# Cached multi-head attention on one core: steps of four heads, two batches at once in the projections, p scaled before a bf16 transpose

## The chip, the core and the metric

The kernel runs on one core of a Trainium2 chip. A core has TensorE (PE, matrix products into PSUM), VectorE (DVE) and ScalarE (ACT) for the work on rows, GpSimd (POOL, here only for an identity matrix), and SyncE (SP), whose queue issues all transfers (DMAs) between the device's memory and the on-chip SBUF. The engines work side by side; each works through its own list in order and waits on semaphores for the others. The metric is the device time of one execution in microseconds (us); lower is better.

## The reference

Eight batches of 112 queries attend to cached keys and values of 32 heads. Keys and values come as they are; q and the output are projected.

```python
B, Sq, D = 8, 112, 640
H, Sk, Dh = 32, 512, 192          # x, k_cache, v_cache, wq, wo are bf16
q = (x @ wq).reshape(B, Sq, H, Dh).transpose(0, 2, 1, 3)
scores = einsum("bhqd,bhkd->bhqk", q, k_cache) * (Dh ** -0.5)
p = softmax(scores, axis=-1)
o = einsum("bhqk,bhkd->bhqd", p, v_cache)
return o.transpose(0, 2, 1, 3).reshape(B, Sq, H * Dh) @ wo     # (8, 112, 640)
```

## The kernel before

**Tiling.** The heads are taken in four groups of eight (HG = 8), and one group of one batch is a *unit*: 32 units, group by group, batch by batch. A unit's keys arrive by a transposing DMA in `kt` (three buffers), its values by a plain DMA in `vt` (three buffers), each 1536 KB. Four keys at a time lie in one row of 768 numbers, so that a head's 192 channels are cut at 128-channel borders: chunk 0 holds channels 0 to 127 of the even keys, chunk 2 channels 64 to 191 of the odd keys, and chunk 1 the last 64 of the even ones in its lower half beside the first 64 of the odd ones in its upper half. A unit is worked off in four *pairs* of heads, 128 pairs in all.

**A pair's stages.** On PE: Q (L210, fifteen products of 112 columns, one batch), S (L137 to L140: per head four products of 256 columns; for chunk 1, L138 and L140, the q operand has zeros in the other half's rows, so each is a full product), PT0 and PT1 (L153: p transposed by a product with a diagonal matrix `dg` that holds 1/sum, so that p is normalised in the same product; output f32), PV (L171 for 128 channels of each head, L178 for the other 64 of both heads, side by side in the two column halves of the array), O (L194 and L195: o as weights, `wo` as the moving operand of 512 and 128 columns, accumulated over a unit in PSUM). On DVE: smax (L265, scaled copy of the scores with the row minimum of their negative), qc (L256 to L259, four copies that arrange q for the chunks), the evacuation of the second transposed p (L271), recip (L277), two diag (L249), and once a unit the sum over head groups (L291 to L295). On ACT: the evacuation of q (L220), of the first transposed p (L226), the two exps (L232, with the row sums), the evacuation of o (L239).

**Order.** `DEFAULT_ORDERS` gives each engine's list of stages with lags: in iteration i PE does S of pair i, PT of pair i−1, PV of pair i−2, O of pair i−3 and Q of pair i+2. SP issues per unit K, V and one weight load (L336, L344, L354 or L361; 480 KB), each K and V after the unit three back has given up its buffer; x comes batch by batch (L347). The last eight units have no weight load behind them. The outputs are stored at the end (L396).

Of the kernel before, what the change touches and what calls it, by code (L numbers as in the profile page):

```python
# [11 lines left out]
DEFAULT_ORDERS = dict(  # L12
    PE=[("S", 0), ("PT0", -1), ("PV", -2), ("PT1", -1), ("O", -3), ("Q", 2)],
    ACT=[("evacQ", 1), ("evacpT0", -1), ("exp0", 0), ("exp1", 0), ("evacPV", -2)],
    DVE=[("smax0", 0), ("smax1", 0), ("qc", 1), ("evacpT1", -1), ("recip", 0), ("diag0", 0), ("diag1", 0),
         ("oacc", -3)],
)


def build_mha_kernel(nc, x, k_cache, v_cache, wq, wo, out, cfg=None):  # L20
    cfg = dict(cfg or {})
    B, SQ, D = x.shape
    _, H, SK, DH = k_cache.shape
    assert SQ == 112 and D == 640 and SK == 512 and DH == 192
    assert H % 4 == 0
    HD = H * DH
    DC = D // 128
    HG = cfg.get("HG", 8 if H % 8 == 0 else 4)
    assert H % HG == 0 and HG % 4 == 0
    NHG = H // HG  # L30
    PPU = HG // 2
    NUNIT = NHG * B
    NPAIR = NUNIT * PPU
    scale = float(DH) ** -0.5

    def unit_of(ip):
        u, lp = divmod(ip, PPU)
        hg, b = divmod(u, B)
        return u, hg, b, lp

    NB = 3
    NQ = cfg.get("NQ", 3)
    NSS = cfg.get("NSS", 4)
    NP = cfg.get("NP", 4)
    ND = cfg.get("ND", 4)
    NPT = cfg.get("NPT", 3)
    NO = cfg.get("NO", 3)
    NS = 8
    QJ = [0, 2, 1, 3]
    orders = dict(DEFAULT_ORDERS)  # L50
    orders.update(cfg.get("orders", {}))
    lags = [lag for o in orders.values() for _, lag in o]
    PER = range(-max(lags), NPAIR - min(lags))

    EA = [0, 5]
    OC = [4, 2]
    ET = [7, 6]
    OH = [3, 8]
    NSLOT = 9

    with ExitStack() as es:
# [3 lines left out]
        def sem(name):  # L65
            return es.enter_context(nc.semaphore(name))

        WQC = HG * DH
        wq_sb = sb("wq_sb", [128, 2, DC, WQC], BF16)
        wo_sb = sb("wo_sb", [128, 2, 3 * PPU, D], BF16)  # L70
        acc = sb("acc", [SQ, B, D], F32)
# [3 lines left out]
        qs = sb("qs", [128, NQ, NSLOT, SQ], BF16)  # L75
        s_sb = sb("s_sb", [SQ, NSS, SK], F32)
        p_sb = sb("p_sb", [SQ, NP, SK], BF16)
        dg = sb("dg", [SQ, ND, SQ], BF16)
        pT_sb = sb("pT_sb", [128, NPT, 2, 4 * SQ], BF16)
        oT_sb = sb("oT_sb", [128, NO, 3, SQ], BF16)  # L80
        o_out = sb("o_out", [SQ, B, D], BF16)
        ident = sb("ident", [128, 128], BF16)
        nmx = sb("nmx", [SQ, NS], F32)
        rsum = sb("rsum", [SQ, NS], F32)
        rinv = sb("rinv", [SQ, NS], F32)
        ps = es.enter_context(nc.psum_tensor("ps", [128, 8, 512], F32))

        sS = sem("sS"); sPT = sem("sPT"); sPV = sem("sPV"); sO = sem("sO"); sQ = sem("sQ")
        dSM = sem("dSM"); dDG = sem("dDG"); dQC = sem("dQC"); dPTE = sem("dPTE"); dOA = sem("dOA"); dRC = sem("dRC")
        aEX = sem("aEX"); aQE = sem("aQE"); aPTE = sem("aPTE"); aPVE = sem("aPVE")  # L90
        gI0 = sem("gI0"); gINIT = sem("gINIT"); dINIT = sem("dINIT")
        mX = [sem(f"mX{j}") for j in range(B)]
        dummy = sb("dmy_act", [SQ, 4], F32)
        mK = [sem(f"mK{j}") for j in range(NB)]
        mV = [sem(f"mV{j}") for j in range(NB)]
        mK0 = sem("mK0b"); mV0 = sem("mV0b")
        mOUT = [sem(f"mOUT{j}") for j in range(2)]

        mWQ = [sem(f"mWQ{j}") for j in range(3 * PPU)]
        mWO = [sem(f"mWO{j}") for j in range(3 * PPU)]  # L100

        def wsem(lst, hg, lp):
            return lst[lp if hg == 0 else (1 + hg % 2) * PPU + lp]

        def wcount(hg):
            return 16 if hg == 0 else 16 * ((hg + 1) // 2)

        HALF = PPU // 2

        def kv_wait(eng, sems, first2, u, lp):  # L110
            if u == 0 and lp >= HALF:
                W(eng, first2, 16)
            else:
                W(eng, sems[u % NB], 16 * (u // NB + 1))

        block = es.enter_context(nc.Block())

        def W(eng, s, v):
            if v > 0:
                eng.wait_ge(s, v)  # L120

        def ok(ip):
            return 0 <= ip < NPAIR

        def pe_S(pe, i):
            u_, hg, b, lp = unit_of(i)
            qb = i % NQ
            W(pe, dQC, i + 1)
            kv_wait(pe, mK, mK0, u_, lp)
            for h in range(2):  # L130
                Hh = 2 * i + h
                u = Hh % HG
                W(pe, dSM, Hh - 1)
                bk = ps[0:SQ, h, :]
                ktb = kt[u_ % NB]
                cs = slice(u * 128, (u + 1) * 128)
                pe.matmul(bk[:, 0:256], qs[:, qb, EA[h], :], ktb[:, :, 0, cs], start=True, stop=False)  # L137
                pe.matmul(bk[:, 0:256], qs[:, qb, ET[h], :], ktb[:, :, 1, cs], start=False, stop=True)  # L138
                pe.matmul(bk[:, 256:512], qs[:, qb, OC[h], :], ktb[:, :, 2, cs], start=True, stop=False)  # L139
                pe.matmul(bk[:, 256:512], qs[:, qb, OH[h], :], ktb[:, :, 1, cs], start=False, stop=True).then_inc(sS, 1)  # L140

        def pe_PT(pe, ip, h):
            Hh = 2 * ip + h
            W(pe, aEX, Hh + 1)
            W(pe, dDG, Hh + 1)
            if h == 0:
                W(pe, aPTE, ip)
            else:
                W(pe, dPTE, ip)
            pslot = Hh % NP  # L150
            dslot = Hh % ND
            for j in range(4):
                mm = pe.matmul(ps[:, 2 + h, j * SQ:(j + 1) * SQ], p_sb[:, pslot, j * 128:(j + 1) * 128],  # L153
                               dg[:, dslot, :], start=True, stop=True)
            mm.then_inc(sPT, 1)

        def pe_PV(pe, ip):
            u_, hg, b, lp = unit_of(ip)
            ptb = ip % NPT
            W(pe, aPTE, ip + 1)  # L160
            W(pe, dPTE, ip + 1)
            kv_wait(pe, mV, mV0, u_, lp)
            W(pe, aPVE, ip)
            vtb = vt[u_ % NB]
            for h in range(2):
                u = 2 * lp + h
                oc = 0 if h == 0 else 2
                for j in range(4):
                    q = QJ[j]
                    d0 = q * 192 + 64 * h  # L170
                    pe.matmul(ps[:, 4, oc * SQ:(oc + 1) * SQ], vtb[:, u, d0:d0 + 128],  # L171
                              pT_sb[:, ptb, h, j * SQ:(j + 1) * SQ], start=(j == 0), stop=(j == 3))
            for j in range(4):
                q = QJ[j]
                for h in range(2):
                    u = 2 * lp + h
# [5 lines left out]
        def pe_O(pe, ip):  # L182
# [3 lines left out]
            if b == 0:  # L186
                W(pe, wsem(mWO, hg, lp), wcount(hg))
# [261 lines left out]
```

## Time and profile before

| | |
|---|---|
| median of 3 runs (lowest to highest) | 499.33 us (498.08 to 499.46) |
| the profiled execution, its own time | 501.18 us |
| its span on the engines | 499.4 us, granted PE clock 0.999 |
| DVE smax L265 | 256 of 686 ns |
| ACT exp L232 | 256 of 711 ns |
| DVE cast L271, 128x448 f32 to bf16 | 128 of 625 ns |
| DVE diag L249, 112x112 | 256 of 248 ns |
| DVE copies L256 and L257, 64x112 and 64x336 | 128 each of 179 and 243 ns |
| first and last scores on PE | start at 13.47 and 486.42 us |
| landing after issue, median: K, V, weights | 14.8, 8.3, 8.8 us |

How to read it: the page of a profile gives busy shares by engine, the span in 40 slices, the *chain that ended last* (followed back from the last instruction to whatever released each step), groups of like instructions with their mean duration and the idle time in front of them, and the DMA issues. The trace gives single instructions: start, length, engine, line, operation, output<-input, shape, and in brackets the idle time before it with what ended it; "x8" means eight merged in one row. A matmul's length is modelled and includes its way through the array, so matmuls overlap and the distance between two starts is the better measure of what one costs.

### The profile page before, as it was taken

The page shows a single profiled execution, that of the slowest core. Times are in us where ns is not written, and L with a number is a line of the kernel's source. Part 1 is how long each engine was busy: PE and PEld are TensorE (multiplying, and loading weights), DVE is VectorE, ACT ScalarE, POOL GpSimd, SP SyncE. Part 2 cuts the span into 40 slices and gives each one's busy share as a digit, 9 for nine tenths or more (in the row PEclk, how much of TensorE's full clock was granted, in tenths as well). Part 3 has the DMA queues.
Part 4 walks back from the last instruction along what each step waited for, and adds up shares of the span by engine and source line. Part 5 has one row for each costly group of instructions (what it writes and reads, how often), then busy time and mean ns, then how long its engine had stood idle before and what let it go on. Part 6 is the DMA issues. An engine that isn't in the chain of part 4 may idle for free.

```text
span 499.4 us, 18328 instructions
## 1 busy us (share of the span) xinstructions
PE 474.5 (95%) x6784; PEld 414.9 (83%) x6784; DVE 441.7 (88%) x1602; ACT 355.2 (71%) x898; POOL 0.7 (0%) x6
## 2 busy tenths in 40 slices
PE   1688999999989999999999999999999999999996
PEld 1677888888878888888888888888888888888884
DVE  1488999999989999999999999999999999999994
ACT  1366777777776777777777777777777777777773
POOL 0000000000000000000000000000000000000000
PEclk9999999999999999999999999999999999999999
DMA  7999999999999999999999999999999999978000
GB/s 202 304 280 238 273 266 248 281 262 202 286 261 270 280 298 244 302 259 285 270 237 254 265 265 278 240 279 267 270 271 262 236 213 219 249 208 238 2 15 24
DMA packets 253703, 119.86 MB, mean 240 GB/s; under 512 B 203568, under 2 KB 253616, under 8 KB 253616
## 3 DMA queue, kind: packets, MB, share of 16 engines
q1 hardware_dynamic: 253616, 118.70, 104.4%
q8 instruction: 55, 0.90, 0.7%
q14 instruction: 32, 0.26, 0.2%
HBM read 66.06 MB, written 1.15 MB: 135 GB/s over the span
## 4 chain that ended last, share of the span: by engine, by line
PE 93%; SPq 3%; issue 2%; DVE 1%; DMA 1%; ACT 0%; DVEq 0%; ACTq 0%
PE ps L210 19%; PE ps L194 16%; PE ps L153 13%; PE ps L171 10%; PE ps L178 8%; PE ps L137 6%; PE ps L138 6%; PE ps L140 6%; PE ps L139 6%; PE ps L195 4%; SPq L336 2%; DMA wq_sb<-in_wq_dram 1%; DVE s_sb L265 0%; SPq L347 0%; SPq L354 0%
## 5 line engine op out<-in xcount | busy, mean ns | idle before, releaser
L265 DVE TENSOR_SCALAR_CACHE_REDUCE s_sb<-ps 112x512 f32<-112x512 f32 x256 | 166.3, 686 | 23.8 <-PE ps L140 21.8
L232 ACT ACTIVATE p_sb<-s_sb,nmx 112x512 bf16<-112x512 f32 x256 | 181.4, 711 | 2.8 <-DVE s_sb L265 2.0
L210 PE MATMUL ps<-xT_sb,wq_sb 128*128 128x112 bf16 x1920 | 117.5, 215 | 14.7 <-DMA wq_sb<-in_wq_dram 14.7
L226 ACT ACTIVATE pT_sb<-ps 128x448 bf16<-128x448 f32 x128 | 69.6, 544 | 85.2 <-PE ps L153 85.2
L210 PEld LDWEIGHTS ps<-xT_sb,wq_sb 128*128 128x128 bf16 x1920 | 103.3, 99 | 25.9 <-DMA wq_sb<-in_wq_dram 8.7
L194 PE MATMUL ps<-wo_sb,oT_sb 128*112 128x512 bf16 x384 | 118.3, 380 | 0.0
L153 PE MATMUL ps<-dg,p_sb 112*128 112x112 bf16 x1024 | 94.1, 214 | 1.9 <-ACT p_sb L232 1.4
L220 ACT ACTIVATE qs<-ps 128x336 bf16<-128x336 f32 x128 | 57.7, 451 | 48.3 <-PE ps L210 44.6
L271 DVE CAST pT_sb<-ps 128x448 bf16<-128x448 f32 x128 | 80.0, 625 | 6.3 <-PE ps L153 2.4
L195 PE MATMUL ps<-wo_sb,oT_sb 128*112 128x128 bf16 x384 | 83.9, 219 | 0.0
L153 PEld LDWEIGHTS ps<-dg,p_sb 112*128 112x128 bf16 x1024 | 64.7, 98 | 14.4 <-ACT p_sb L232 1.6
L137 PE MATMUL ps<-kt,qs 128*112 128x256 bf16 x256 | 70.8, 277 | 2.9 <-issue 2.9
L171 PE MATMUL ps<-pT_sb,vt 128*128 128x112 bf16 x1024 | 71.8, 213 | 1.4 <-issue 1.3
L138 PE MATMUL ps<-kt,qs 128*112 128x256 bf16 x256 | 70.4, 275 | 0.2 <-issue 0.2
L140 PE MATMUL ps<-kt,qs 128*112 128x256 bf16 x256 | 70.4, 275 | 0.0
L139 PE MATMUL ps<-kt,qs 128*112 128x256 bf16 x256 | 70.4, 275 | 0.0
L194 PEld LDWEIGHTS ps<-wo_sb,oT_sb 128*112 128x112 bf16 x384 | 49.7, 129 | 22.3
L171 PEld LDWEIGHTS ps<-pT_sb,vt 128*128 128x128 bf16 x1024 | 56.6, 98 | 2.2 <-issue 1.8
L249 DVE TENSOR_SCALAR dg<-ident,rinv 112x112 bf16<-112x112 bf16 x256 | 52.7, 248 | 5.1 <-issue 0.6
L239 ACT ACTIVATE oT_sb<-ps 128x336 bf16<-128x336 f32 x128 | 55.3, 432 | 2.0 <-PE ps L178 2.0
L178 PE MATMUL ps<-pT_sb,vt 128*64 128x112 bf16 x1024 | 49.8, 219 | 0.4 <-issue 0.4
L195 PEld LDWEIGHTS ps<-wo_sb,oT_sb 128*112 128x112 bf16 x384 | 50.0, 130 | 0.0
(25 smaller groups left out, 397.2 us busy)
## 6 DMA issues: line engine op xcount, KB each, us to landing
vt<-in_v_cache_dram SPq DMA_DIRECT2D x31, 1536.0 KB, 8.3
wq_sb<-in_wq_dram SPq DMA_DIRECT2D x16, 480.0 KB, 8.8
wo_sb<-in_wo_dram SPq DMA_DIRECT2D x16, 480.0 KB, 8.8
vt<-in_v_cache_dram SPq DMA_DIRECT2D x2, 768.0 KB, 7.1
out_dram<-o_out SPq DMA_DIRECT2D x8, 140.0 KB, 4.7
kt<-in_k_cache_dram SPq DMA_TRANSPOSE x33, 14.8
xT_sb<-in_x_dram SPq DMA_TRANSPOSE x8, 8.9
```

The lines of the kernel that those rows point to most:

```text
L137: pe.matmul(bk[:, 0:256], qs[:, qb, EA[h], :], ktb[:, :, 0, cs], start=True, stop=False)
L138: pe.matmul(bk[:, 0:256], qs[:, qb, ET[h], :], ktb[:, :, 1, cs], start=False, stop=True)
L139: pe.matmul(bk[:, 256:512], qs[:, qb, OC[h], :], ktb[:, :, 2, cs], start=True, stop=False)
L140: pe.matmul(bk[:, 256:512], qs[:, qb, OH[h], :], ktb[:, :, 1, cs], start=False, stop=True).then_inc(sS, 1)
L153: mm = pe.matmul(ps[:, 2 + h, j * SQ:(j + 1) * SQ], p_sb[:, pslot, j * 128:(j + 1) * 128], dg[:, dslot, :], start=True, stop=True)
L171: pe.matmul(ps[:, 4, oc * SQ:(oc + 1) * SQ], vtb[:, u, d0:d0 + 128], pT_sb[:, ptb, h, j * SQ:(j + 1) * SQ], start=(j == 0), stop=(j == 3))
L178: mm = pe.matmul(ps[64 * h:64 * h + 64, 4, SQ:2 * SQ], vtb[:, u, d0:d0 + 64], pT_sb[:, ptb, h, j * SQ:(j + 1) * SQ], start=(j == 0), stop= ...
L194: pe.matmul(ps[0:SQ, 6, :], oT_sb[:, ob, c, :], wo_sb[:, wb, 3 * lp + c, 0:512], start=first, stop=last)
L195: mm = pe.matmul(ps[0:SQ, 7, 0:128], oT_sb[:, ob, c, :], wo_sb[:, wb, 3 * lp + c, 512:640], start=first, stop=last)
L210: mm = pe.matmul(ps[:, 5, c * SQ:(c + 1) * SQ], lhsT, xT_sb[:, dc, b * SQ:(b + 1) * SQ], start=(dc == 0), stop=(dc == DC - 1))
L232: act.activation(p_sb[:, Hh % NP, :], s_sb[:, Hh % NSS, :], ACTF.Exp, bias=nmx[:, Hh % NS:Hh % NS + 1], scale=-1.0, accum_out=rsum[:, Hh % ...
L265: dve.tensor_scalar(s_sb[:, Hh % NSS, :], ps[0:SQ, h, :], -scale, None, op0=ALU.mult, op1=ALU.min, accum_out=nmx[:, Hh % NS:Hh % NS + 1]). ...
```

## The change

The kernel is written anew around a small class `Plan`, in which each operation is added with the operations that it depends on, and each engine gets a list of operations in the order written by hand; waits follow from both. The parts:

- **Step of four heads.** A step n is half a unit (64 steps). Two units with the same head group and neighbouring batches form a *tile* t of four steps; the first tile alternates between its batches, the others do a whole unit before the next.
- **q for two batches** (`q_fill`): the fifteen products have 224 columns, once for two batches, one such group a step. ACT writes them to `qr`; DVE makes two copies per step (`qc`, 64 rows of 2x3x112 each) to the other half of the rows in `qh`. No zeros are needed.
- **Scores** (`scores`): chunks 0 and 2 as before; chunk 1 by two products of 64 rows each, in the two row halves of the array and into two PSUM banks. Even keys of two heads lie in one bank, odd keys in the next, four banks for a step.
- **Normalising on p** (`norm`, DVE, 112x512 bf16 in place), then PE transposes in bf16 into a bf16 PSUM bank (`transposes`), evacuated by one DVE copy of 128x896 for two heads (`evPT`). `dg` and ACT's evacuation of p go.
- **P·V** (`values`): the same products for four heads, rests first; one ACT evacuation for four heads.
- **Output projection transposed** (`o_half`): `wo` as weights, o of two batches as the moving operand of 224 columns, over twelve pieces of 128 rows into one bank, four fills a tile, one in each step, each added to `accT` by DVE. At the end the sums are transposed back by PE (`o_final`), copied by ACT and stored; the last tile's projection is done per batch.
- **Loads**: two units' keys, then two units' values, then two of the next weights; x in three loads (two, two and four batches).

The core of the diff, new lines:

```diff
+        def qc(n):
...
+            def emit(e):
+                e.tensor_copy(qh[64:128, n % 2, :, 0:3, :], src[0:64])
+                return e.tensor_copy(qh[0:64, n % 2, :, 1:4, :], src[64:128])
...
+            for j in range(2):
+                def emit(e, j=j):
+                    for h in range(2):
+                        i = 2 * j + h
...
+                        e.matmul(ps[0:SQ, 2 * j, hs], ev, ktb[:, :, 0, cs(i)], start=(h == 0), stop=False,
+                                 skip_group_check=True)
+                        mm = e.matmul(ps[0:SQ, 2 * j + 1, hs], od, ktb[:, :, 2, cs(i)], start=(h == 0), stop=False,
+                                      skip_group_check=True)
+                    return mm
+                add("PE", ("Sm", n, j), [("qc", n), k_of(n), ("smax", n - 1, 2 * j), ("smax", n - 1, 2 * j + 1)], emit)
...
+                    m1 = e.matmul(ps[0:SQ, 2 * j, hs], ev, ktb[0:64, :, 1, cs(i)], start=False, stop=True,
+                                  skip_group_check=True)
+                    m2 = e.matmul(ps[0:SQ, 2 * j + 1, hs], od, ktb[64:128, :, 1, cs(i)], start=False, stop=True,
+                                  skip_group_check=True)
...
+                def norm(e, i=i, k=k):
+                    return e.tensor_scalar(p_sb[:, i, :], p_sb[:, i, :], rinv[:, k:k + 1], None, op0=ALU.mult)
+                add("DVE", ("smax", n, i), [("St", n, 2 * j + 1), ("exp", n - 1, i)], smax)
+                add("ACT", ("exp", n, i), [("smax", n, i), ("PT", n - 1, j)], exp)
+                add("DVE", ("norm", n, i), [("rc", n, j)], norm)
...
+            def evac(e):
+                return e.tensor_copy(pT_sb[:, (2 * n + j) % NPT, :, :].rearrange("p h c -> p (h c)"),
+                                     psb[:, 4 + j, 0:8 * SQ])
...
+            add("PE", ("PT", n, j), [("norm", n, 2 * j), ("norm", n, 2 * j + 1), ("evPV", n - 1)], emit)
+            add("DVE", ("evPT", n, j), [("PT", n, j), ("PVm", m // 2, m % 2)], evac)
...
+                for j, m, k in todo:
+                    mm = e.matmul(ps[:, 7, j * S2:(j + 1) * S2], wo_sb[:, hg % 2, k, m * 128:(m + 1) * 128],
+                                  oT_sb[:, t % 2, k, :], start=(k == 0), stop=(k == 3 * LP - 1))
```

The order lists of the engines, for step n (loads at the start, then the steady part of SP):

```diff
+            if n >= 5 and n + 3 < NG:
+                pe += [("Qb", n + 3)]
+                act += [("evQb", n + 3)]
+            if n:
+                pe += [("PT", n - 1, 1)]
+            pe += [("Sm", n, 0), ("Sm", n, 1)] + [("St", n, i) for i in range(4)]
+            if n:
+                pe += [("PVt", n - 1), ("PVm", n - 1, 0), ("PVm", n - 1, 1)]
+            pe += late[:2]
+            if n >= 4 and n + 4 < NG:
+                pe += [("Qa", n + 4)]
...
+            pe += [("PT", n, 0)] + late[2:]
...
+            pe += [("O", t, f, 1) for t, f in o_now[-1:]]
+            act += [("exp", n, 0), ("exp", n, 1)]
+            if n:
+                act += [("evPV", n - 1)]
...
+            act += [("exp", n, 2), ("exp", n, 3)]
...
+            if n >= 4 and n + 4 < NG:
+                act += [("evQa", n + 4)]
+            dve += [("oacc", t, f) for t, f in o_step(n - 1)[-1:]]
+            if n:
+                dve += [("evPT", n - 1, 1)]
+            if n + 1 < NN and n != 1:
+                dve += [("qc", n + 1)]
+            dve += [("smax", n, i) for i in range(4)]
...
+            dve += [("rc", n, 0), ("norm", n, 0), ("norm", n, 1), ("evPT", n, 0), ("rc", n, 1), ("norm", n, 2),
+                    ("norm", n, 3)]
...
+        load_k(("K", 2), 2, 0, HG, "mK2", kd(2))
+        load_x(2, 4, 8)
+        load_v(("V", 2), 2, 0, HG, "mV2", vd(2))
+        for lp in range(LP):
+            load_wo(0, lp)
+        load_k(("K", 3), 3, 0, HG, "mK0", kd(3))
+        load_v(("V", 3), 3, 0, HG, "mV0", vd(3))
+        for t in range(2, NT):
+            for u in (2 * t, 2 * t + 1):
+                load_k(("K", u), u, 0, HG, f"mK{u % NB}", kd(u))
...
+            for u in (2 * t, 2 * t + 1):
+                load_v(("V", u), u, 0, HG, f"mV{u % NB}", vd(u))
```

## The prediction, made before the changed kernel was run

> **What bounds the kernel now.** I read first the page's busy shares, the chain of work that ended last and the DMA row:
>
> ```profile
> PE 474.5 (95%) x6784; PEld 414.9 (83%) x6784; DVE 441.7 (88%) x1602; ACT 355.2 (71%) x898; POOL 0.7 (0%) x6
> ...
> DMA  7999999999999999999999999999999999978000
> ...
> PE 93%; SPq 3%; issue 2%; DVE 1%; DMA 1%; ACT 0%; DVEq 0%; ACTq 0%
> ```
>
> TensorE (PE) ends the run, but VectorE (DVE) is only 7 points behind, and the DMA engines are full until slice 37. So a gain on PE soon meets DVE or the DMA. How much room there is shows in one period of the timeline, PE's rows first (start, length, what):
>
> ```profile
> 249.77 0.28 PE L137 MATMUL ps<-kt,qs 128*112 128x256 bf16 x1
> ...
> 250.54 0.27 PE L140 MATMUL ps<-kt,qs 128*112 128x256 bf16 x1
> 250.65 0.36 PE L153 MATMUL ps<-dg,p_sb 112*128 112x112 bf16 x4
> 250.85 0.56 PE L171 MATMUL ps<-pT_sb,vt 128*128 128x112 bf16 x8
> 251.34 0.39 PE L178 MATMUL ps<-pT_sb,vt 128*64 128x112 bf16 x8
> 251.66 0.37 PE L153 MATMUL ps<-dg,p_sb 112*128 112x112 bf16 x4
> 251.87 0.38 PE L194 MATMUL ps<-wo_sb,oT_sb 128*112 128x512 bf16 x1
> ...
> 252.68 0.90 PE L210 MATMUL ps<-xT_sb,wq_sb 128*128 128x112 bf16 x15
> 253.42 0.28 PE L137 MATMUL ps<-kt,qs 128*112 128x256 bf16 x1
> ```
>
> L137 comes back after 253.42 − 249.77 = 3.65 us: a pair of heads. PE never waits in it: scores 0.88 (8 of 0.11), p transposes 2 x 0.20, P·V mains 0.39, rests 0.20, output projection 0.81, q 0.74, and about 0.11 before and after L178, where the 64-column weights begin and end (L171's eight at 0.049 are through at 251.24, L178 starts at 251.34). The run is 13.5 us until the first scores, 127 x 3.65 = 463.5, 9.4 of stalls on the way (the last scores start at 486.4) and 13.0 from there to the end. DVE in the same period:
>
> ```profile
> 251.03 0.69 DVE L265 TENSOR_SCALAR_CACHE_REDUCE s_sb<-ps 112x512 f32<-112x512 f32 x1
> 251.64 0.08 DVE L265 DVE_READ_ACCUMULATOR s_sb<-ps 112x1 f32 x1
> 251.64 0.18 DVE L256 COPY qs<-qs 64x112 bf16<-64x112 bf16 x1
> 251.83 0.24 DVE L257 COPY qs<-qs 64x336 bf16<-64x336 bf16 x1
> 252.09 0.24 DVE L258 COPY qs<-qs 64x336 bf16<-64x336 bf16 x1
> 252.34 0.19 DVE L259 COPY qs<-qs 64x112 bf16<-64x112 bf16 x1
> 252.56 0.63 DVE L271 CAST pT_sb<-ps 128x448 bf16<-128x448 f32 x1
> 253.22 0.17 DVE L277 RECIPROCAL rinv<-rsum 112x2 f32<-112x2 f32 x1
> 253.42 0.41 DVE L249 TENSOR_SCALAR dg<-ident,rinv 112x112 bf16<-112x112 bf16 x2
> ```
>
> It has next to no gaps either: every price below is a distance between two of these starts.
>
> **The change, PE.** For four heads, before 7.30. Now: q 15 matmuls of 224 columns (twice L210's 112: 0.095) = 1.42; transposes 16 x 0.049 = 0.79; full scores 8 x 0.109 = 0.87; the 64-row rest of the scores as four pairs, 0.44 if the two row halves run side by side as L178's two column halves do (8 in 0.20), 0.87 if not; rests 0.39; mains 0.79; output projection 15 x 0.095 = 1.42; three changes of tile shape x 0.11 = 0.33. Sum 6.45, or 6.9. By PE alone the change would save 64 x 0.85 = 54 us.
>
> **The change, DVE.** In: norm (4 x 112x512 bf16), evPT (2 x 128x896 from bf16 PSUM), qc (2 copies of 64x672), a 224- or 448-wide add. Out: diags, the old evacuation, four small copies a pair. ScalarE loses the evacuation of L226 (128 x 0.54) and gains nothing long: exps 4 x 0.70, evPV 0.77 (L239's 336 columns in 0.43, L226's 448 in 0.54: 1 ns a column), evQ 0.54 + 0.33 make 4.4 a step. Prices, as distances start to start:
> - smax: 251.03 to 251.64 = 0.61, so four 2.46 (two banks instead of one change nothing in the count).
> - reciprocal to the scaled rows: 253.22 to 253.42 = 0.20.
> - norm: not in the trace. The nearest row is L249 (112x112, mean 248 ns, two in 0.41, so 0.16 apart). Copies L256 and L257 take 179 and 243 ns for 112 and 336 elements: 224 more in 64 ns, 3.5 a ns. The missing 400 elements cost 0.10 at the copies' rate, and the pair 0.41 + 0.21 = 0.62; at half that rate 0.83; at one element per 1.04 ns (L265: 512 in about 0.53) 1.24. From below, at the copies' price 0.29 each with the overlap of L249, 0.45. I take 0.62: same operation as L249, same memory as the copies.
> - evPT: no bf16 read of PSUM in the trace. L271 moves the same bytes (448 f32) in 0.625, 0.66 to the next op; one element per 1.04 ns would make it 1.09. I take 0.66, nearest in bytes and place.
> - qc: L257 to L258 is 0.26 for 336; 672 makes 0.34, two 0.68 (1.7 if one element at a time; the copies exclude it).
>
> **What decides: the order of DVE's list.** It runs in order, and a step now reads: add, evPT(n-1,1), qc(n+1), smax x4, rc, norm, norm, **evPT(n,0)**, rc, norm, norm. Each evPT reads transposes that need the norms directly in front of it. So DVE stands twice a step for a round trip through PE: norm to PE 0.08 (diag to L153 takes 0.07 to 0.10 where PE waits, at 490.75 and 491.07), eight transposes 7 x 0.049 + 0.21 = 0.56, PE to DVE 0.04 (L140 ends 250.37, L265 starts 250.41): 0.68. The second trip hides the add (0.39 to 0.62); the first hides nothing, and rc, two norms and the next smax are queued behind. In the kernel before, the CAST comes after other work and waited 2.4 us in all. The loop:
>
> 2.46 + 0.20 + 0.62 + 0.68 + 0.66 + 0.20 + 0.62 + 0.68 + 0.66 + 0.68 = **7.46 us** a step, against 7.30.
>
> Others beside it, counted from smax's start: the fourth exp's sum at about 4.4 (0.74 + 2 x 0.70 + 0.77 + 0.70 + 0.81), while DVE asks at 4.6; PE is back at the first transposes after 2.9 to 3.5, while the norms end at 3.3, so it mostly idles there; q's second half waits for ACT's copy behind the fourth exp and ends about when the second norms do, 5.4; PE's own path from the second transposes to the next scores is 0.39 + 0.87 + 0.11 + 0.22 + 0.2 = 1.8, DVE's 0.60 + 0.66 + 0.68 = 1.94. Score halves not side by side add 0.2 to the former: +0.1 a step. These margins are narrow; none gives time back.
>
> Two rules of the Trainium skill speak here. "VectorE: DVE Perf Modes", section The DRAIN you can't avoid, lets the next instruction start only when the pipe is empty: norm pairs would cost 0.70, the loop +0.17, the run +10 us; L249's two in 0.41 with 0.248 each disagree. Its tier table gives bf16 tensor_scalar in SBUF 4x and bf16 from PSUM 2x, by which evPT is about 0.63 and the loop stays as it is; no run here shows that yet.
>
> **DMA.** SP's K issues of 122.33 to 257.91 are ten in 135.6, 13.56 a unit of K, V and one weight load (3552 KB): 3.82 us per 1000 KB, with SP never idle. At two steps a unit the DMA can feed 6.78 a step, so it is no bound at 7.46, but would be at PE's 6.45. K(2t+1) waits for scores two units back and V(2t) is queued behind it; counted from the scores that free K(2t)'s slot, a unit later (14.9) and one K issue (7) V goes out at 22, lands 8.3 later (median of the page) and is wanted after 2.5 units, 37: some 7 to spare.
>
> Start, by these rates (x 1.1 a batch, from six units of 14.65 at 34.42 to 122.33): the same sum puts the old K of unit 2 at 48.3, and PE waited for it until 49.30. Two batches' x, two weight loads and half a K land at 11.5; q takes PE's slow first stretch and qc 0.7, so scores start near 12.6. K of unit 3 now lies behind x of four batches, V and four output weights and lands at 67.4, where step 6 would have wanted it at 62. V of unit 4 costs some 3.5 more, units 1 and 2 some 4. I count 13 us of stalls, against 9.4.
>
> End, from the last scores' start: 1.4 to smax, 5.4 to the last norm, 0.68, 0.66, P·V 1.6, copy 0.8, last output half 1.7, adds 0.9, transposes 0.5, copy 0.75, store 2.5 (as before, 496.9 to 499.4): 16.9 against 13.0. Two late steps with doubled output halves: +1.
>
> **Sum**, on the profiled span of 499.4: first scores −0.9, stalls +3.6, 63 x 7.46 − 127 x 3.65 = +6.4, doubled steps +1, tail +3.9: 513.4. That execution took 501.18 in all, the median of the runs is 499.33; the two offsets cancel, so I forecast **513 us**. One tenth of a us in the loop is 6 us.
>
> **Rivals.**
> 1. *The loop as priced*, 0.60: 500 to 525.
> 2. *DVE prices of the dearer kind*, 0.16. Norm at half the copies' rate: loop +0.42, 539. EvPT at one element: +0.86, 567. For: neither is in the trace. Against: the copies' rate.
> 3. *Faster: the loop shorter than its parts*, 0.19. Norm pairs at 0.45 and trips at 0.55 give 6.86 and 475 us; below 6.78 the DMA takes over, near 470. It decides from a loop of 7.23 on. For: L249's overlap is large. Against: the trips rest on observed starts.
> 4. *No change*, 0.05: a loop of about 7.2.
> That the halves of the scores run one after another lies inside 1 (+6).
>
> Chances, with 0.3% as what measurement can tell from no change: faster 0.19, same 0.05, slower 0.76. The range: 494 leaves out most of rival 3, 541 takes in norm at half rate.
>
> **What would show it.** Right: norm rows near 350 ns, evPT near 625; DVE idle before evPT(n,0), released by the transposes, some 0.68 x 64 = 43 us; PE near 6.45 of 7.46 busy; a step of 7.3 to 7.6. Wrong: PE or the DMA on the last chain with DVE idle of a few us (rival 3); evPT near 1.09 or norm near 450 (rival 2).

## The result: 3.3% slower

The changed kernel takes **515.34 us** (median of 4 runs, 514.60 to 517.11); the kernel before took 499.10 on the same chip (498.08 to 499.46). The ratio is 1.033, with an interval of 1.030 to 1.037. The profiled execution took 515.33 us, its span is 513.5.

The page of the changed kernel, the lines that answer to those of before:

```profile
PE 451.4 (88%) x6116; PEld 384.5 (75%) x6116; DVE 401.1 (78%) x1217; ACT 283.8 (55%) x714; POOL 0.7 (0%) x6
...
DMA  8999999999999999999999979798997959592101
...
PE 47%; ACT 26%; DVE 9%; SPq 9%; issue 5%; DMA 4%; DVEq 0%
ACT p_sb L300 19%; PE ps L224 9%; DVE s_sb L295 7%; PE ps L320 7%; PE ps L377 7%; SPq L117 6%; PE ps L282 6%; PE ps L270 5%; PE ps L272 5%; ACT oT_sb L362 3%; ACT qr L230 3%; PE ps L354 3%; DMA kt<-in_k_cache_dram 3%; PE ps L343 2%; SPq L131 2%
```

PE, DVE and ACT are all less busy than before, and the run is longer: the time went into waits of the engines for each other. The DMA row has gaps from slice 24 on, and the steps there are as long as the steps before it (7.40 to 7.43, see below), so the DMA doesn't bound the step either. The chain is split among PE, ACT and DVE; by itself it doesn't say which of them to relieve. It suggests ScalarE's exps (L300), and this reading was tested below as the rival.

One step of four heads on DVE, from one first row maximum (L295) to the next (left out: the other three with their accumulator reads, the reciprocals, and q's copies at 262.38 and 262.72). The bracket is the idle time before the row and what ended it:

```profile
255.67 0.69 DVE L295 TENSOR_SCALAR_CACHE_REDUCE s_sb<-ps 112x512 f32<-112x512 f32 x1
...
258.44 0.62 DVE L304 TENSOR_SCALAR p_sb<-p_sb,rinv 112x512 bf16<-112x512 bf16 x2
259.72 0.62 DVE L325 COPY pT_sb<-ps 128x896 bf16<-128x896 bf16 x1 [0.66 <-PE ps L320]
...
260.45 0.62 DVE L304 TENSOR_SCALAR p_sb<-p_sb,rinv 112x512 bf16<-112x512 bf16 x2
260.98 0.39 DVE L395 TENSOR_TENSOR accT<-ps,accT 128x224 f32<-128x224 f32 x1
261.73 0.62 DVE L325 COPY pT_sb<-ps 128x896 bf16<-128x896 bf16 x1 [0.36 <-PE ps L320]
...
263.08 0.69 DVE L295 TENSOR_SCALAR_CACHE_REDUCE s_sb<-ps 112x512 f32<-112x512 f32 x1
```

The step is 263.08 − 255.67 = 7.41 (7.40 to 7.43 wherever no load is waited for). The two round trips stand in it as priced: the norms end at 259.06 and 261.07, the copies start 0.66 later; the first trip is empty, the add covers 0.30 of the second (0.36 of it is idle). Term by term, as distances from start to start (from an end to the next start for the trips):

| term | predicted | measured |
|---|---|---|
| four row maxima | 2.46 | 2.57 |
| reciprocal, two norms | 0.20, 0.62 | 0.20, 0.62 |
| first trip, copy | 0.68, 0.66 | 0.66, 0.54 |
| reciprocal, two norms | 0.20, 0.62 | 0.19, 0.62 |
| second trip, copy | 0.68, 0.66 | 0.66, 0.65 |
| q's two copies | 0.68 | 0.70 |

The two that miss, +0.11 and −0.12, cancel. The last row is not DVE's alone: 0.10 of it is a wait for PE, as experiment 2 shows. The unknown operations came out at the value taken, as the groups show (after the bar busy us and mean ns, then idle before):

```profile
L325 DVE COPY pT_sb<-ps 128x896 bf16<-128x896 bf16 x128 | 79.9, 624 | 66.7 <-PE ps L320 64.6
...
L304 DVE TENSOR_SCALAR p_sb<-p_sb,rinv 112x512 bf16<-112x512 bf16 x256 | 78.9, 351 | 4.5
```

But "as priced" is not yet "this is what binds". The PE rows of the same step, and the wait for the scores, hold a detail that decided the first experiment:

```profile
261.12 0.57 PE L320 MATMUL ps<-ident,p_sb 112*128 112x112 bf16 x8
...
262.65 0.27 PE L284 MATMUL ps<-kt,qr 64*112 64x256 bf16 x1
```

The first row maximum needs the score pair that starts at 262.65; its modelled end is 262.92, and the maximum starts at 263.08, 0.16 after. Where a full-array product releases the maximum, in the kernel before, it is 0.04. This points to the scores as what releases it, and not DVE's own list; the row has no wait bracket that would tell. Experiment 1 settles it: there DVE waits for these scores in the open, and the maximum again starts 0.16 after the pair's end.

### The profile page after: what moved, and what is told of

It is laid out like the page before. It is cut to its first block, busy times and chain, and to the rows that moved or that the text cites. A ratio compares the mean times of both kernels' runs of the same rounds, so it can differ in the third digit from the quotient of the medians.

```text
span 513.5 us, 14612 instructions
## 1 busy us (share of the span) xinstructions
PE 451.4 (88%) x6116; PEld 384.5 (75%) x6116; DVE 401.1 (78%) x1217; ACT 283.8 (55%) x714; POOL 0.7 (0%) x6
## 3 DMA queue, kind: packets, MB, share of 16 engines
HBM read 66.06 MB, written 1.15 MB: 131 GB/s over the span
## 4 chain that ended last, share of the span: by engine, by line
PE 47%; ACT 26%; DVE 9%; SPq 9%; issue 5%; DMA 4%; DVEq 0%
ACT p_sb L300 19%; PE ps L224 9%; DVE s_sb L295 7%; PE ps L320 7%; PE ps L377 7%; SPq L117 6%; PE ps L282 6%; PE ps L270 5%; PE ps L272 5%; ACT oT_sb L362 3%; ACT qr L230 3%; PE ps L354 3%; DMA kt<-in_k_cache_dram 3%; PE ps L343 2%; SPq L131 2%
## 5 line engine op out<-in xcount | busy, mean ns | idle before, releaser
L300 ACT ACTIVATE p_sb<-s_sb,nmx 112x512 bf16<-112x512 f32 x256 | 181.9, 712 | 161.3 <-DVE s_sb L295 161.3
L295 DVE TENSOR_SCALAR_CACHE_REDUCE s_sb<-ps 112x512 f32<-112x512 f32 x256 | 161.5, 687 | 10.2 <-PE ps L284 8.7
L325 DVE COPY pT_sb<-ps 128x896 bf16<-128x896 bf16 x128 | 79.9, 624 | 66.7 <-PE ps L320 64.6
L224 PE MATMUL ps<-xT_sb,wq_sb 128*128 128x224 bf16 x960 | 113.6, 262 | 17.6 <-ACT qr L230 10.3
L377 PE MATMUL ps<-oT_sb,wo_sb 128*128 128x224 bf16 x900 | 105.3, 259 | 1.8 <-DMA wo_sb<-in_wo_dram 1.8
L320 PE MATMUL ps<-ident,p_sb 112*128 112x112 bf16 x1024 | 73.1, 215 | 31.3 <-DVE p_sb L304 29.7
L320 PEld LDWEIGHTS ps<-ident,p_sb 112*128 112x128 bf16 x1024 | 53.8, 98 | 56.8 <-DVE p_sb L304 54.3
L230 ACT ACTIVATE qr<-ps 128x448 bf16<-128x448 f32 (+1 forms) x128 | 56.0, 441 | 56.3 <-PE ps L224 55.9
L377 PEld LDWEIGHTS ps<-oT_sb,wo_sb 128*128 128x128 bf16 x900 | 83.7, 98 | 2.0 <-issue 2.0
L304 DVE TENSOR_SCALAR p_sb<-p_sb,rinv 112x512 bf16<-112x512 bf16 x256 | 78.9, 351 | 4.5
L300 ACT ACTIVATION_READ_ACCUMULATOR p_sb<-s_sb,nmx 112x1 f32 x256 | 48.2, 188 | 0.0
L270 PE MATMUL ps<-kt,qr 128*112 128x256 bf16 x128 | 35.8, 279 | 5.4 <-DMA kt<-in_k_cache_dram 3.5
L272 PE MATMUL ps<-kt,qr 128*112 128x256 bf16 x128 | 35.5, 277 | 0.0
L270 PE MATMUL ps<-kt,qh 128*112 128x256 bf16 x128 | 35.4, 277 | 0.0
L272 PE MATMUL ps<-kt,qh 128*112 128x256 bf16 x128 | 35.4, 276 | 0.0
```

The source lines that it names most:

```text
L224: mm = e.matmul(ps[:, bank, j * S2:(j + 1) * S2], wq_sb[:, hg % 2, dc, c0:c0 + 128], xT_sb[:, dc, bp * S2:(bp + 1) * S2], start=(dc == 0), ...
L230: return e.activation(qr[:, t % 2, lp, blocks[0]:blocks[0] + n, :], ps[:, bank, 0:n * S2].rearrange("p (c s) -> p c s", c=n), ACTF.Copy)
L270: e.matmul(ps[0:SQ, 2 * j, hs], ev, ktb[:, :, 0, cs(i)], start=(h == 0), stop=False, skip_group_check=True)
L272: mm = e.matmul(ps[0:SQ, 2 * j + 1, hs], od, ktb[:, :, 2, cs(i)], start=(h == 0), stop=False, skip_group_check=True)
L295: return e.tensor_scalar(s_sb[:, i, :].rearrange("p (e c) -> p e c", e=2), ps[0:SQ, 2 * j:2 * j + 2, h * 256:(h + 1) * 256], -scale, None, ...
L300: return e.activation(p_sb[:, i, :], s_sb[:, i, :], ACTF.Exp, bias=nmx[:, k:k + 1], scale=-1.0, accum_out=rsum[:, k:k + 1])
```

## The experiments

Theory A is throughout the loop of DVE's list with its two trips through PE. Theory B is the chain's reading, ScalarE's list. Other letters are explained where they stand.

### 1. The first trip filled

```diff
-            if n + 1 < NN and n != 1:
-                dve += [("qc", n + 1)]
             dve += [("smax", n, i) for i in range(4)]
...
-            dve += [("rc", n, 0), ("norm", n, 0), ("norm", n, 1), ("evPT", n, 0), ("rc", n, 1), ("norm", n, 2),
-                    ("norm", n, 3)]
+            dve += [("rc", n, 0), ("norm", n, 0), ("norm", n, 1)]
+            if n + 1 < NN and n != 1:
+                dve += [("qc", n + 1)]
+            dve += [("evPT", n, 0), ("rc", n, 1), ("norm", n, 2), ("norm", n, 3)]
```

> One line moves: VectorE's two q copies (0.68 us) go from in front of the row maxima into the gap between the first two norms and the first evacuation of transposed p. Theory A (VectorE's list with two round trips through TensorE sets the step of 7.41 us): the gap of 0.66 is filled, but the second norms then gate the second transposes, and the next scores lie behind those on TensorE: from the norms' end, 5.40 after the first row maximum, 0.05, transposes 0.40, scores 1.43 give 7.28. So only 0.13 a step comes back: about 506 us of span, 507 to 508 device time. Theory B (the page's chain: exps, the o and q evacuations on ScalarE, then the second half of q on TensorE set the step): nothing on that chain moves, 515. Theory C (a filled gap is worth its length): 6.75 a step, about 475.

Measured: 514.76 us (513.94 to 515.89), 1.031 of before (1.026 to 1.037), no gain. The step stays 7.41, every fourth one 7.49. DVE's waits in this kernel (what waits and for whom: us in all, times, longest):

```profile
DVE s_sb L295 <- PE ps L284: 48.2, 63, 1.8
DVE pT_sb L325 <- PE ps L320: 22.7, 52, 1.6
```

In the changed kernel the same two lines read 8.7 and 64.6: the idle time moved from the copies to the row maximum, and its sum hardly fell (73.3 to 70.9). The norms of a step end at 259.07; then PE's second transposes, and the next row maximum on DVE:

```profile
259.14 0.57 PE L320 MATMUL ps<-ident,p_sb 112*128 112x112 bf16 x8
261.10 0.69 DVE L295 TENSOR_SCALAR_CACHE_REDUCE s_sb<-ps 112x512 f32<-112x512 f32 x1 [0.73 <-PE ps L284]
```

From the transposes' start to this row maximum it is 1.96: transposes 0.40, full scores 0.97, the pair's start 0.15, its length 0.27, its release 0.16. From the first maximum to the end of the norms it is 5.39 with the trip filled as with the trip empty (5.40), since the copy behind it waits for the transposes either way. 5.39 + 0.07 + 1.96 = 7.42. **The transposes stand ahead of the next scores in PE's list, and so both lists are in one loop**; q's copies were beside it. Of Theory A the size fell here: it had put this path at 0.40 + 1.43 = 1.83. The 515 of Theory B came out, so this run alone does not decide between the two; the next ones do.

### 2. The add taken out of the second trip

```diff
-            dve += [("oacc", t, f) for t, f in o_step(n - 1)[-1:]]
             if n:
                 dve += [("evPT", n - 1, 1)]
+            dve += [("oacc", t, f) for t, f in o_step(n - 1)[-1:]]
```

> One line moves: the add of the output projection (0.39 or 0.62 us, one a step) goes from the second round trip, where it hides, to behind the second evacuation. Theory A: the trip of 0.66 is then empty and the add is paid on top: 7.41 + 0.42 to 0.65, on average 0.47, a step from step 6 on: about 540 us. Theory B (chain over ScalarE): the add is not on it, 515.

Measured: 523.99 us, 1.049 (1.043 to 1.056). The steps are 7.59, or 7.82 with the wide add. The end of a step on DVE, q's second copy and the next row maximum:

```profile
264.48 0.33 DVE L248 COPY qh<-qr 64x672 bf16<-64x672 bf16 x1
264.74 0.68 DVE L295 TENSOR_SCALAR_CACHE_REDUCE s_sb<-ps 112x512 f32<-112x512 f32 x1
```

From the copy of the transposes to the add it is 0.54 (263.19 to 263.73), from there to q's first copy 0.41: 0.95 for the 0.65 without the add. But from q's second copy to the maximum it is 0.26 for 0.36 (262.72 to 263.08 above), and that is the measure of DVE's slack: in the changed kernel DVE could have started the maximum 0.10 earlier. So DVE's own list is 7.31 long, PE's branch makes it 7.41, and 0.30 more of DVE work costs 0.30 − 0.10 = 0.2 a step. Work in the second trip is hidden work, as A says, but with less effect than expected: I had forgotten that margin, and that the distance behind a copy is not constant (0.54 here, 0.65 in the changed kernel). Theory B's 515 is missed by 9 us: the add is not on its chain.

### 3. The last third of q behind the scores, besides experiment 1

```diff
-            if n >= 5 and n + 3 < NG:
-                pe += [("Qb", n + 3)]
-                act += [("evQb", n + 3)]
             if n:
                 pe += [("PT", n - 1, 1)]
             pe += [("Sm", n, 0), ("Sm", n, 1)] + [("St", n, i) for i in range(4)]
+            if n >= 5 and n + 3 < NG:
+                pe += [("Qb", n + 3)]
+                act += [("evQb", n + 3)]
```

> e1, and TensorE's second half of q goes from in front of the second transposes to behind the scores, so that ScalarE's q evacuation no longer stands in front of the transposes. Theory A: norms, second transposes, scores remain the loop, 7.28 to 7.4 a step, so 506 to 514, no better than e1. Theory B: the wait of TensorE for ScalarE's q copy (0.17 a step, and the 0.48 of these products) leaves the chain, 6.8 to 7.1 a step, 478 to 497.

Measured: 526.85 us, 1.055 (1.049 to 1.061), slower than both theories allow; steps of 7.50 and, every fourth, 8.08. B falls: ScalarE's copy behind the exps no longer stands ahead of the second transposes, and nothing was gained. PE now stands idle for 0.99 in front of them, until DVE's norms are done:

```profile
273.39 0.57 PE L320 MATMUL ps<-ident,p_sb 112*128 112x112 bf16 x8 [0.99 <-DVE p_sb L304]
```

In the changed kernel, too, they start 0.05 behind these norms (261.12 after 261.07). What was lost is on PE: q now stands ahead of the first transposes.

```profile
270.52 0.62 DVE L304 TENSOR_SCALAR p_sb<-p_sb,rinv 112x512 bf16<-112x512 bf16 x2
...
271.27 0.56 PE L320 MATMUL ps<-ident,p_sb 112*128 112x112 bf16 x8
```

The norms end at 271.14, the transposes start 0.13 later instead of 0.05 (the step is 0.09 longer); in the step with 24 output products, twelve of them ahead of the transposes, 0.7 later. The prediction said that PE "mostly idles" ahead of these transposes; the room was about 0.4 us in three steps and none in the fourth.

### 4. The next scores ahead of the second transposes, work in both trips

On PE the scores of step n go ahead of the second transposes of n−1, on DVE the first row maximum ahead of the copy that waits for them, and q's copies into the first trip. (PE does q's first part ahead of P·V, ACT copies it behind the first exp, both output halves go ahead of the first transposes, the add to the end of the step.)

```diff
+            pe += [("Sm", n, 0), ("Sm", n, 1)] + [("St", n, i) for i in range(4)]
             if n:
                 pe += [("PT", n - 1, 1)]
-            pe += [("Sm", n, 0), ("Sm", n, 1)] + [("St", n, i) for i in range(4)]
...
+            dve += [("smax", n, 0)]
             if n:
                 dve += [("evPT", n - 1, 1)]
-            if n + 1 < NN and n != 1:
-                dve += [("qc", n + 1)]
-            dve += [("smax", n, i) for i in range(4)]
+            dve += [("smax", n, i) for i in range(1, 4)]
...
+            dve += [("rc", n, 0), ("norm", n, 0), ("norm", n, 1)]
+            if n + 1 < NN and n != 1:
+                dve += [("qc", n + 1)]
+            dve += [("evPT", n, 0), ("rc", n, 1), ("norm", n, 2), ("norm", n, 3)]
```

> The same instructions in another order: TensorE does the next step's scores before the second transposes, q's first half in the wait for their evacuation and both output halves before the first transposes; VectorE does one row maximum in the second round trip and the q copies in the first; ScalarE copies q between the first two exps. Theory A: with both trips filled VectorE needs 2.46 + 0.2 + 0.62 + 0.68 + 0.65 + 0.2 + 0.62 + 0.45 + 0.65 = 6.5 a step, TensorE 6.45, and while weights are loaded the DMA engines feed 6.78: 6.6 to 6.8 a step, 475 to 482 us, faster than both kernels. If TensorE's or ScalarE's amount of work or something unseen (the row-halved scores, bank conflicts) set the step, the order changes little: above 500.

Measured: **479.64 us** (479.27 to 480.47), 0.961 (0.957 to 0.965): 36 us less than the changed kernel and faster than the kernel before, with the same instructions. Where no load is waited for, steps are 6.34 to 6.37, every fourth 7.49. On DVE in one step, the first norms and copy, and the next first row maximum with the copy behind it; then PE's three groups of transposes (first of a step, second, first of the next):

```profile
331.23 0.62 DVE L304 TENSOR_SCALAR p_sb<-p_sb,rinv 112x512 bf16<-112x512 bf16 x2
...
332.56 0.62 DVE L325 COPY pT_sb<-ps 128x896 bf16<-128x896 bf16 x1
...
334.40 0.69 DVE L295 TENSOR_SCALAR_CACHE_REDUCE s_sb<-ps 112x512 f32<-112x512 f32 x1
335.01 0.62 DVE L325 COPY pT_sb<-ps 128x896 bf16<-128x896 bf16 x1
```

```profile
331.97 0.56 PE L320 MATMUL ps<-ident,p_sb 112*128 112x112 bf16 x8
332.36 0.65 PE L224 MATMUL ps<-xT_sb,wq_sb 128*128 128x224 bf16 x5
...
334.39 0.57 PE L320 MATMUL ps<-ident,p_sb 112*128 112x112 bf16 x8
...
338.31 0.56 PE L320 MATMUL ps<-ident,p_sb 112*128 112x112 bf16 x8
```

Both copies follow the work in front of them without a bracket, q's copies (331.88 to 332.56) in the first trip, the add and the row maximum in the second. PE goes from one group to the next: first transposes 0.39, end of q 0.48, scores 1.55, second transposes 0.40, q 1.05, P·V 0.52 and 0.80, output 1.15, together 6.34: PE waits for nothing in this step, and its list is what bounds it now. ACT's share rose to 61%, and it waits 129 us ahead of the exps: not the bound.

### 5 and 6. One half of it taken back at a time

In experiment 5 q's copies go back ahead of the reciprocal, so that only the first trip is empty again; in 6 the copy of the second transposes goes back ahead of all row maxima, so that only the second one is. PE's and ACT's lists stay as in 4.

```diff
+            if n + 1 < NN and n != 1:
+                dve += [("qc", n + 1)]
             dve += [("rc", n, 0), ("norm", n, 0), ("norm", n, 1)]
-            if n + 1 < NN and n != 1:
-                dve += [("qc", n + 1)]
             dve += [("evPT", n, 0), ("rc", n, 1), ("norm", n, 2), ("norm", n, 3)]
```

```diff
-            dve += [("smax", n, 0)]
             if n:
                 dve += [("evPT", n - 1, 1)]
-            dve += [("smax", n, i) for i in range(1, 4)]
+            dve += [("smax", n, i) for i in range(4)]
```

> The version with the next scores ahead of the second transposes and both trips filled (step 6.34, 479.6 us), with one thing taken back: q's two copies stand ahead of the reciprocal instead of in the first trip. The same instructions, only the trip is empty again. Theory A (an empty trip costs its length, because DVE's list is in order and has no other slack): DVE's list was full at 6.34, now the trip of 0.68 stands empty in it, so three steps of four go to 6.95 to 7.05; the fourth, with 24 output products, was bound by PE at 7.49 and goes to 7.5 to 7.7. 48 x 0.66 + 16 x 0.1 = +33, less up to 12 us of stalls for keys and values that vanish at the slower pace: 498 to 513 us. Rival C (only the place of the scores in PE's list mattered, the trips are free): 479 to 483 us, step 6.34 to 6.40. Rival B (ScalarE's chain sets the step): 479 to 483 us as well, ACT's list is untouched.

> The version with the next scores ahead of the second transposes and both trips filled (step 6.34, 479.6 us), with the other thing taken back: the copy of the second transposed p stands ahead of all four row maxima again instead of behind the first. In PE's list these transposes stay behind the next scores. Theory A: DVE now waits for them with nothing in front but the add; in the 479.6 us version they start when the first row maximum does and are through 0.62 later, so DVE idles 0.6 a step more: 6.9 to 7.0 in three steps, 7.5 to 8.1 in the fourth, 500 to 518 us less some stalls, so 498 to 515. Rival C (the place of the scores in PE's list is all that mattered): 479 to 483 us.

Measured: 504.92 us, 1.011 (1.005 to 1.016), and 504.94 us, 1.011 (1.007 to 1.014); steps of 7.11 and 7.15, every fourth 7.49 in both. Experiment 5:

```profile
339.71 0.62 DVE L325 COPY pT_sb<-ps 128x896 bf16<-128x896 bf16 x1 [0.66 <-PE ps L320]
```

Experiment 6:

```profile
342.61 0.62 DVE L325 COPY pT_sb<-ps 128x896 bf16<-128x896 bf16 x1 [0.66 <-PE ps L320]
```

The runs are as long as expected, the steps a little longer than the 6.9 to 7.05 of Theory A. They grew by 0.77 and 0.81: each empty trip costs its 0.66, and 0.11 and 0.15 come behind it (DVE then waits 0.19 for the scores in 5, 0.18 for the exps in 6). In the run that is 25 us, for either trip. So the place of the scores in PE's list does not do it alone, and ScalarE's list, which is the same in 4, 5 and 6, does not set the step. The whole of experiment 4 is worth 36 us, where filling the first trip with PE's order unchanged (experiment 1) was worth nothing. PE's new order with both trips empty was not run.

### 7. The steady loads in the order K, V, K, V, weights

```diff
-            for u in (2 * t, 2 * t + 1):
-                load_k(("K", u), u, 0, HG, f"mK{u % NB}", kd(u))
...
-            for hg, lp in wq_now:
-                load_wq(hg, lp)
             for u in (2 * t, 2 * t + 1):
+                load_k(("K", u), u, 0, HG, f"mK{u % NB}", kd(u))
                 load_v(("V", u), u, 0, HG, f"mV{u % NB}", vd(u))
+            for hg, lp in wq_now:
+                load_wq(hg, lp)
```

> The changed kernel with only the order of the steady loads undone: K, V, K, V, then the two weights, instead of K, K, weights, V, V, weights. Theory A (DVE's loop of 7.41 sets the step and the DMA could feed 6.78): nothing in the steady part, 513 to 517 us, steps 7.40 to 7.43. Rival D (the order of the loads is part of the loss, values come late): 505 to 512 us, with fewer and shorter waits at the first scores of a unit.

Measured: 513.14 us (512.76 to 515.05), 1.028 (1.024 to 1.032); the steps are 7.40 to 7.43 to the end. The 2 us are at the start: step 6, which waits for the keys of unit 3 (issued ahead of the lines changed), starts at 65.05 instead of 66.23, and step 7 at 74.04 instead of 76.13. In experiments 1, 2, 3 and 8, which have the changed kernel's list of loads, these starts lie anywhere from 63.98 to 65.57 and from 71.44 to 75.21. So the 2 us are within the scatter there, and the order of the loads is no part of the loss that these runs can show.

### 8. The end of the lists

```diff
-        pe += [("OL", 0, 0), ("OL", 0, 1), ("PT", n - 1, 1), ("OF", B - 2), ("OL", 1, 0), ("PVt", n - 1),
-               ("PVm", n - 1, 0), ("PVm", n - 1, 1), ("OL", 1, 1), ("OF", B - 1)]
+        pe += [("OL", 0, 0), ("PT", n - 1, 1), ("OL", 0, 1), ("PVt", n - 1), ("PVm", n - 1, 0),
+               ("PVm", n - 1, 1), ("OL", 1, 0), ("OL", 1, 1), ("OF", B - 2), ("OF", B - 1)]
...
-        dve += [("oaccL", 0), ("evPT", n - 1, 1), ("oaccL", 1)]
+        dve += [("evPT", n - 1, 1), ("oaccL", 0), ("oaccL", 1)]
```

> The changed kernel with only the end of PE's, ACT's and DVE's lists reordered: first half of batch 6's last projection, second transposes of step 63, second half of batch 6, P.V of step 63, both halves of batch 7, then both transposes of sums; DVE's copy of the transposes ahead of the sum of batch 6. Theory A: in the changed kernel the transposes of step 63 stood 1.2 us behind 60 products (norms ended 500.83, they started 502.07) and P.V behind 30 more products and a transpose. Now they start at 500.9 and PE runs without a gap: 0.4 + 90 products of 0.05 + P.V 1.2 = 6.1 to the end of the last half at 507.0 against 508.9. From the last scores' start to the end 17.5 to 18.1 instead of 19.9, 512 to 514.5 us. Rival: the store and the copies bound the tail anyway, 19.5 or more, 514 to 516 us.

The end as it is in the changed kernel:

```profile
499.12 3.11 PE L409 MATMUL ps<-oT_sb,wo_sb 128*128 128x112 bf16 x60
...
502.07 0.56 PE L320 MATMUL ps<-ident,p_sb 112*128 112x112 bf16 x8
```

and reordered:

```profile
499.13 0.57 PE L320 MATMUL ps<-ident,p_sb 112*128 112x112 bf16 x8
499.54 1.64 PE L409 MATMUL ps<-oT_sb,wo_sb 128*128 128x112 bf16 x30
```

The norms end at 500.83 there and 499.07 here, the transposes start 1.24 and 0.06 later. Measured: 512.74 us, 1.026 (1.021 to 1.031), of which the trace gives the edit 1.45: from the last scores to the end 18.49 instead of 19.94. That is less than the 1.8 to 2.4 expected. PE is through with the last half 1.7 earlier (13.7 after the last scores' start, before 15.4), for 1.9 reckoned; about 0.28 is given back because the last transposes now start 0.33 behind the sums instead of 0.05: they wait for ScalarE to copy those of batch 6 out of the same bank.

### 9 to 11. Towards a best version

Experiment 9 is 4 with the end of 8 (batch 6's transposes between the two last halves), 10 adds the loads of 7, 11 splits the 24 output products of every fourth step around the first transposes:

```diff
+            split = len(o_now) == 1 and o_now[0][1] == 1
-            pe += [("O", t, f, h) for t, f in o_now[:1] for h in range(2)]
+            pe += [("O", t, f, h) for t, f in o_now[:1] for h in range(1 if split else 2)]
             pe += [("PT", n, 0)] + late[2:]
+            pe += [("O", t, f, 1) for t, f in o_now[:1] if split]
```

> The 479.6 us version (next scores ahead of the second transposes, both trips filled) with the end of the lists reordered as in the tail experiment, and the transposes of batch 6's sums between the two last halves. Theory A: the tail's gain is the same piece of PE queue, 1.5 to 2.0 us: 477.3 to 478.5 us, from the last scores' start to the end 18.4 to 19.0 instead of 20.5. Rival: something else ends the run, 479 to 480.

> The version before it in this list, with the steady loads in the order K, V, K, V, weights. The order made nothing of the changed kernel, whose step of 7.41 left the DMA time. At steps of 6.34 and 7.49 (mean 6.63) P.V waited for values in three steps (1.0 to 1.8 us on PE, steps longer by 1.1 to 3.8). Theory D: the values are late because they are queued behind the second K, which waits for its buffer; with V ahead of it these waits go: 4 to 8 us less, 470 to 474 us. Rival: the DMA's rate is the bound at this pace (6.78 a step with weights), the waits only move to the keys: 476 to 479 us.

> The version before it in this list, and in the step with 24 output products the second twelve go behind the first transposes. In the 479.6 us version these steps are 7.49, of which 0.19 is more than PE's own list (6.16 + 12 x 0.095 = 7.30), because the transposes come late and DVE idles 1.16 for them. Theory: the fourth step goes to 7.3, 15 x 0.19 = 3 us less than the version before it. Rival: the products only move in front of the next scores, which DVE then waits for: no change within 1 us, or the DMA takes the gain.

Measured side by side: 478.75 us (476.44 to 479.93), 0.958 (0.954 to 0.962); **474.09** (471.46 to 474.96), 0.950 (0.946 to 0.954); 473.82 (470.84 to 474.65), 0.948 (0.943 to 0.952). In 9 the end is 1.2 shorter by the trace (19.26 for 20.49), less than the 1.5 to 2.0 expected, and the runs don't separate 9 from 4. In 9 PE waits for values:

```profile
PE ps L343 <- DMA vt<-in_v_cache_dram: 7.4, 5, 2.8
```

In 10 there is no such wait; steps 10, 14, 22, 26 and 38, which took 7.27 to 10.87 in 9, take 6.34. The same edit that did nothing at a step of 7.41 is worth 4.7 us at 6.6. The split of 11 does nothing, as its rival said: the fourth step stays 7.49, DVE's wait moves from the copy to the row maximum (0.97). PE's own list has that length there: 6.34 with twelve output products, 12 x 0.095 = 1.14 more with 24.

## Why the prediction was right, and where it was not

**The sign and the size** came from one step, the loop through DVE's list: 7.46 predicted, 7.41 measured, against 7.30. That these agree to 0.05 is in part luck: DVE's list by itself is 7.31 (experiment 2), and PE's branch, which the prediction held to be the shorter one, adds the other 0.10. With 7.31 the run would be some 6 us shorter, by 63 x 0.10, and still slower than before. Norm (351 ns), copy (624 ns) and trips (0.66) came out as chosen, so rival 2 (dearer operations) and rival 3 (cheaper ones) are out: no price had to give. The rule that would have made the loop 0.17 longer (the Trainium skill, "VectorE: DVE Perf Modes", section "The DRAIN you can't avoid") does not hold for these rows: the pair of norms takes 0.62 from the first start to the last end, at 0.351 each. In its section "Two Vector instructions with no wait between them" the same page makes only a held instruction wait for every earlier one to finish; the second norm starts some 0.08 before the first ends (2 x 0.351 − 0.62).

**The span adds up with errors that cancel.** Predicted 513.4, measured 513.5: first scores 13.2 for 12.6 (+0.6), 63 steps 0.05 shorter (−3.2), stalls 11.2 for 13 (−1.8), the last steps with doubled output halves +2.3 for +1 (+1.3), end 19.9 for 16.9 (+3.0). The median is 2.3 above the forecast because the profiled execution lies on the median this time, not 1.85 above it.

**The step that failed is "PE's own path from the second transposes to the next scores is ... 1.8, DVE's 0.60 + 0.66 + 0.68 = 1.94"**, and with it the sentence that DVE's list alone decides. PE's path is 1.96 (0.16 of it from the modelled end of the row-halved products to the start of their reader), DVE's 1.86. On the sum this is 0.1; on what to do about it, it is everything: as long as PE's order ties the second transposes to the next scores, work moved into the first trip wins nothing. The expectation of 1 still had PE's path at 1.83 and 0.13 a step to be won, and missed for that reason. That of 2 missed because 0.10 of DVE's step was a wait for PE, that of 3 because q came to stand ahead of the first transposes.

**The end** was mis-sized by the queue on PE: 60 products (3.0 us) stand ahead of the last step's second transposes, 30 more and a transpose ahead of its P·V. I had reckoned the dependences, not the list. Experiment 8 wins back 1.45 of the 3.0 that the end took beyond the forecast; no run separates the rest.

**PE's list** was 6.45 by the prediction, 6.16 with twelve output products; it is 6.34. The difference is mostly in the changes of tile shape: three at 0.11 were counted, and five places of experiment 4's rows are dearer than their products: from full scores to row halves 0.09, between the first two pairs 0.04, back to full products 0.10, into the 64-column weights 0.10 and out of them 0.13.

**The rival of the chain**: ScalarE's exps hold 19% of the changed kernel's chain, and they are not the bound: in experiment 4 the same exps at the same length allow a step of 6.34, and with that same list on ScalarE an emptied trip on DVE makes it 7.11 or 7.15 (experiments 5 and 6).

Not settled: whether the 0.16 between a row-halved product and its reader belongs to the row halves or to the fact that the reader waits for two products' semaphores; and what makes an instruction's distance to the next vary by 0.11 (the copy to the reciprocal takes 0.54 in the changed kernel and 0.66 in experiment 4, the last maximum to the reciprocal 0.73 and 0.61).

## What to carry to other kernels

Where an engine produces something, another transforms it and the first needs it back, count the round trip once per such pair in the first engine's list, and ask what stands in the list between the two; here a trip filled with other work left no idle time, and an empty one cost its whole length, 0.66 us a step. Before an edit that fills a trip, follow the loop through *both* lists: if the other engine's list ties the trip to the next step's input, one list alone gains nothing, and only the two edits together do. And an order of loads that makes no difference at the slow pace is to be tried again at the fast one.

## What was not expected of the hardware

- The reader of row-halved products (64 rows each, two at once) starts 0.16 us after their modelled end where it waits for them (experiment 1), that of full-array ones 0.04 after (the kernel before).
- The wait for keys at the start of the run scatters by some 2 us: step 6 starts at 66.23 in the changed kernel and at 64.55 in experiment 8, which is the same up to its last step, and with experiments 1, 2 and 3 from 63.98 to 66.23. That is more than anything in the steady part of the changed kernel, where steps repeat within 0.03.
